# A new order for the first 220 tasks of a fused FFT convolution and gated MLP, with later transposes of the inverse tables and another order of staging buffers

## The chip, the cores and the metric

The kernel runs on one core of one Trainium2 chip. The core has a matrix engine (PE), a vector engine (DVE), an activation engine (ACT), a general engine (POOL) and a queue engine (SP) that here does nothing but issue transfers; ACT issues some as well. Each engine works through its own list of instructions in order, and they wait for each other by semaphores. The metric is the device time of one execution in microseconds; the kernel before took 194.77 us (median of three runs).

## The reference

All tensors are bfloat16, with 2048 positions of 512 channels. Two branches work on the same normalised input and are multiplied.

```
x  = A_q;  xn = layernorm(x)
k_shift = sum over t in 0..3 of k moved by t places * shift_k     # 4-tap causal filter per channel
kv = k_shift * v
y  = irfft( rfft(kv, 4096) * rfft(ssm_k, 4096) )[:2048] + kv * ssm_D
s  = xn * y
h  = gelu(xn @ w_gate) * (xn @ w_up)                              # 512 -> 1792
g  = silu(h @ w_down)                                             # 1792 -> 512
out = x + s * g
```

## The kernel before

The long convolution is a discrete Fourier transform in two stages, both done by matrix products. Stage 1 multiplies 128-point tables (F1) with the data, PE's results are evacuated into staging buffers and stored to scratch arrays in DRAM (ZH for the filter ssm_k, ZK for kv). Stage 2 reads them back in another layout (tiles BH and BK), multiplies by a second table (TF) in 32-by-32 blocks (line 1028), multiplies the two spectra (HS, HW), applies the inverse tables (MI, its halves MI0 and MI1, made from TFA and TFB) and goes back through a third scratch array (ZI) to the last stage with the table G1.

The filter is split in two halves. The first, called H in the code, is transposed on PE (line 878, from the tiles Hn) into HTr, and its units 4 to 7 are worked in half pairs of 256 columns. Its evacuated results lie in four quarters of the tile X, which later takes the input, and ACT issues the eight stores. The second half, called J, comes from a permuted copy (HP, by ACT) and a transposing DMA (HTD); SP issues its stores. Its four staging buffers are quarters of X and of G, the tile in which the output is made later. kv is built on DVE: four products of k with the filter taps (lines 1005 and 1009) and three sums (line 1011) for each of four blocks. The taps (SKB) are four copies by POOL out of one loaded tile (SKR).

The MLP works in four quarters of 512 tokens. Each quarter has 14 units; a unit is a gate and an up product (xnT with Wg and Wu), a GELU on ACT (GE, line 1137, or 1128 for a 256-column piece) and a product on DVE (HT, line 1140, or 1130). The first quarter starts with two halves of 256 columns, while weights and input are still landing. The normalised input XN is made on DVE (line 835), transposed on PE (line 854) and evacuated by ACT as xnT (line 609).

The order of all this is written out by hand. Every piece of work is a task with a number, given when it is added. The string SEQ lists 787 places with the numbers, and the planner goes through it exactly in that order and puts each task on the list of its engine. The planner also reckons times from constants (LANDS, W_XT and the costs of the tasks). These times do not change the order. They only decide which slot of a pool of buffers a task gets, by the earliest free one. On the chip an engine waits for semaphores alone.

Loads, stores and transposing transfers issued by SP all stand in one list, so an entry that waits holds up everything behind it. The transposing transfers for G1 and the two tables share one semaphore, so each waits until the one before it has landed. Lines that the prediction names: line 609 is the copy by ACT out of PSUM, line 618 the matmul, line 590 the plain transfer, line 1039 the transposing transfer of the tables.

Of the kernel before, what the change touches and what calls it, by code (L numbers as in the profile page):

```python
# [24 lines left out]
N_WARM = 11  # L25
ORDER = "x02 h0 h1 x22 w0 w1 h2 h3 D0 w2 s0 k0 v0 x1 w3 k1 v1 d0 d1 k2 v2 k3 v3 x2 x3"
SEQ = (
# [22 lines left out]
)  # L50
NF_BANKS = 4
ISSUE = 470.0
LOAD_NS = {("x0_", 262144): 1400.0, ("x0_", 131072): 450.0, 262144: 900.0, 524288: 1350.0, ("x", 524288): 2100.0, ("h", 524288): 1300.0, ("wg", 524288): 1550.0, ("wu", 524288): 1450.0, 917504: 2620.0, ("sk", 524288): 1500.0, 344064: 1250.0, 46080: 350.0, 3072: 100.0, 1024: 200.0}
W_XT, W_SW, W_BK, W_BH, W_ZI, W_BI, W_ZK, W_MI, W_G1 = 1665000, 600000, 555000, 703000, 333000, 640000, 490000, 740000, 222000
NC_PAIRS = 4
SMALL = 1.15 * 262144
T_FWD = 219.0
# [234 lines left out]
class Sched:  # L292
# [8 lines left out]
    FIRST = {"loads": 1050.0, "SP": 30500.0}  # L301
    DRAIN = 121.0
    EARLY, TAKEN, SHARED, WAIT = (0.0, 1.0), 1400.0, 46000.0, 3300.0
    LANDS = (4350.0, 5590.0, 7100.0, 8420.0, 9350.0, 10200.0, 11500.0)

    def __init__(self):
        self.tasks = []
# [37 lines left out]
    def run(self):  # L345
        free = dict(self.FIRST)
        pipe = 0.0
        n_loads = 0
        order = []
        pmode = 0  # L350
        for name in SEQ.split():
            t = self.tasks[int(name.rstrip("b"))]
            eng, dur = t.opts[name[-1] == "b"]
            base = 0.0
            for d in t.deps:
                base = max(base, d.end if eng == d.eng == "PE" else d.end + d.lat + (self.SEM if not d.nbytes or eng != "PE" else 400.0 if d.eng == "loads" else self.HEDGE))
            for b in t.w:
                if b.pool is not None and b.slot is None:
                    f, b.slot = b.pool.find()
                    b.pool.take(b.slot)  # L360
                    base = max(base, f + self.SEM)
            t.start, t.eng = max(base, free.get(eng, 800.0)), eng
            free[eng] = t.end = t.start + dur + (self.DRAIN if eng == "PE" and t.mode != pmode else 0.0)
            pmode = t.mode if eng == "PE" else pmode
            if eng == "loads":
                free[eng] = t.start + dur * (self.EARLY[1] if t.start < self.EARLY[0] else 1.0)
                if n_loads < len(self.LANDS):
                    free[eng] = self.LANDS[n_loads] - self.LOAD_LAT
                n_loads += 1
                t.end = free[eng] + self.LOAD_LAT  # L370
            elif t.nbytes:
                en = t.end
                if en < self.SHARED:
                    free["loads"] += self.TAKEN
                pipe = max(pipe, en + self.DMA_LAT / 2) + t.nbytes / (self.SHARE_BW if en < self.SHARED else self.DMA_BW)
                t.end = pipe + self.DMA_LAT / 2 + (self.WAIT if en < self.SHARED else 0.0)
            for b in set(t.r + t.w):
                b.left -= 1
                b.last_end = max(b.last_end, t.end + t.lat)
                if b.left == 0 and b.pool is not None:  # L380
                    b.pool.release(b.slot, b.last_end)
            order.append(t)
        assert sorted(t.n for t in order) == list(range(len(self.tasks)))
        return order
# [6 lines left out]
def act(n, sb=False):  # L391
    return 170.0 + n * 0.833 + (30.0 if sb else 0.0)


def dve(n, rate):
    return 150.0 + n / 0.96 / rate


def build_kernel(nc, A_q, A_k, A_v, A_shift_k, A_ssm_k, A_ssm_D, B_w_gate, B_w_up, B_w_down, out):
    with ExitStack() as es0:  # L400
# [81 lines left out]
        def quarter(T, j):  # L482
            return T[:, j:j + 2, :].rearrange("p x (y d) -> p (x y) d", d=256).rearrange("p (r c) d -> p r c d", c=2)

        ast = {"H": [quarter(X, j) for j in (8, 10, 12, 14)], "J": [quarter(T, j) for T, j in ((X, 12), (X, 14), (G, 4), (G, 6))],
               "K": [AST[:, j, :, :, :] for j in range(2)] + [ASX[:]]}

        ZH = nc.dram_tensor("ZH", [NG, 128, DM], BF16, kind="Internal")
# [402 lines left out]
        d_htd = [dsem(f"d_htd{hf}") for hf in range(2)]  # L891
        for hf in range(2):
            for k in range(2):
                h_perm.append(op([("ACT", act(1024, True)), ("DVE", dve(1024, 1))], lambda e, h, hf=hf, k=k: copy(e, h, HP[:, 8 * hf:8 * hf + 8, k, :], Hn[:, 2 + k, :].rearrange("p (a t) -> p t a", t=NT)[:, 8 * hf:8 * hf + 8, :]),
                                 r=[bHn[2 + k]], w=[bHP[hf]], rr=[R_Hn[2 + k]], ww=[R_HP[hf]]))
        for hf in range(2):
            def dtr(e, hf=hf):
# [31 lines left out]
        def stage1_h(x, u):  # L929
# [9 lines left out]
            else:  # L939
# [6 lines left out]
                def m(e):  # L946
# [3 lines left out]
                s1_tasks[x].append(S.add([("PE", pe(2))], m, r=[bF1] + bd, w=[p], lat=200.0))  # L950
                form = "p (c d r) -> p r c d" if x == "H" else "p (c r d) -> p r c d"
                op(EV(1024), lambda e, h: copy(e, h, ast[x][a.slot], ps(psl(p)).rearrange(form, c=2, r=2)),
                   r=[p], w=[a], rr=lambda: R_ps[psl(p)], ww=lambda: [R_AST[x][a.slot]], after=[] if x == "H" else zh_tasks["H"])
            zh_tasks[x].append(S.add([("ACT", 350.0) if x == "H" else ("SP", ISSUE)], st, r=[a], w=[bZ["H"][u + (8 if x == "J" else 0)]], nbytes=1.05 * SMALL))

        def stage1_k(u):
# [330 lines left out]
```

## Time and profile before

| what | value |
|---|---|
| three runs | 194.37, 194.77, 195.28 us (median 194.77) |
| span of the profiled execution | 193.3 us; the median of the runs is 1.47 us longer |
| instructions | 3502 |
| PE busy | 188.6 us, 98% of the span |
| DVE busy | 160.0 us, 83% |
| ACT busy | 125.4 us, 65% |
| POOL busy | 13.9 us, 7% |

The profiled execution is one more execution beside the three runs; its page gives its span. A row of a timeline gives the start in us, the time from the start of its first to the end of its last instruction, the engine, the line, the operation, what is written and what is read, and how many instructions there are; brackets give the idle time before it and what ended that. "ACTq" and "SPq" are the issues of transfers on those engines' lists, and the row of a transfer in the list of issues ends with the time from issue to landing. A row of the windows view gives a stretch, then the busy time of PE, weight load, DVE, ACT and POOL in it, the granted clock of PE, the share of the transfer engines and GB/s.

### The profile page before, as it was taken

How to read it: one execution, taken by the hardware profiler on the slowest of the kernel's cores; microseconds unless marked ns; L12 is line 12 of the kernel's file. 1: busy time of each engine (PE TensorE's matmuls, PEld its weight loads, DVE VectorE, ACT ScalarE, POOL GpSimd, SP SyncE). 2: the span in 40 equal slices, each digit the busy share in tenths (PEclk: the TensorE clock that was granted, in tenths of full speed). 3: DMA queues.
4: the chain of work that ended last, by engine and by line, in shares of the span. 5: the costliest groups of instructions: out<-in, count | busy, mean ns of one | idle time of the engine just before them, and what ended most of it. 6: DMA issues, size and time to landing. Idle time of an engine off the chain costs nothing.

```text
span 193.3 us, 3502 instructions
## 1 busy us (share of the span) xinstructions
PE 188.6 (98%) x1377; PEld 85.6 (44%) x1377; DVE 160.0 (83%) x245; ACT 125.4 (65%) x170; POOL 13.9 (7%) x32
## 2 busy tenths in 40 slices
PE   7899999999999999999999999999999999999993
PEld 2685544444444444443434433433444334444452
DVE  6699789998999995877888789878897863588993
ACT  6787999969885987868548766856577431232121
POOL 5412420000000000020300000000000000000000
PEclk9999999999999999999999999999999999999999
DMA  5999999999999679999999991984805345939333
GB/s 175 311 307 349 377 400 347 157 249 372 375 374 354 196 264 259 390 323 305 218 285 230 338 320 59 288 276 147 264 10 195 106 140 153 389 112 353 132 139 136
DMA packets 45958, 49.19 MB, mean 254 GB/s; under 512 B 12787, under 2 KB 39671, under 8 KB 45942
## 3 DMA queue, kind: packets, MB, share of 16 engines
q1 hardware_dynamic: 37366, 42.67, 70.1%
q10 hardware_dynamic: 8576, 6.29, 10.3%
q8 instruction: 11, 0.18, 0.4%
q14 instruction: 5, 0.04, 0.1%
HBM read 27.39 MB, written 14.68 MB: 218 GB/s over the span
## 4 chain that ended last, share of the span: by engine, by line
PE 93%; DMA 4%; SPq 1%; DVE 1%; ACT 0%; issue 0%
PE psall L618 86%; PE psall L1028 5%; DMA Hn<-in_A_ssm_k_dram 4%; PE psall L854 1%; SPq L590 1%; PE psall L878 1%; DVE G L1175 0%; DVE G L1174 0%; ACT G L1172 0%
## 5 line engine op out<-in xcount | busy, mean ns | idle before, releaser
L618 PE MATMUL psall<-xnT,Wu 128*128 128x512 bf16 (+1 forms) x232 | 55.8, 372 | 0.0
L618 PE MATMUL psall<-xnT,Wg 128*128 128x512 bf16 (+1 forms) x232 | 55.3, 372 | 0.0
L618 PE MATMUL psall<-Wd,HT 128*128 128x512 bf16 (+2 forms) x238 | 52.0, 367 | 0.0
L1140 DVE TENSOR_TENSOR HT<-psall,GE 128x512 bf16<-128x512 f32 x54 | 36.7, 685 | 15.8 <-PE psall L618 15.4
L1137 ACT ACTIVATE GE<-psall 128x512 bf16<-128x512 f32 x54 | 31.7, 601 | 13.1 <-PE psall L618 12.9
L618 PEld LDWEIGHTS psall<-Wd,HT 128*128 128x128 bf16 x238 | 22.4, 98 | 25.9 <-issue 1.1
L618 PEld LDWEIGHTS psall<-xnT,Wg 128*128 128x128 bf16 x232 | 21.9, 98 | 25.4 <-issue 1.3
L618 PEld LDWEIGHTS psall<-xnT,Wu 128*128 128x128 bf16 x232 | 21.6, 98 | 25.9 <-issue 3.5
L609 ACT ACTIVATE X<-psall 128x1024 bf16<-128x1024 f32 (+1 forms) x18 | 15.1, 843 | 3.3 <-DMA ZH<-X 1.9
L609 ACT ACTIVATE HS<-psall 128x1024 bf16<-128x1024 f32 x14 | 13.7, 1022 | 4.4 <-PE psall L1028 4.4
L1164 ACT ACTIVATE G<-psall 128x512 bf16<-128x512 f32 x12 | 7.0, 598 | 12.9 <-PE psall L618 12.4
L1011 DVE TENSOR_TENSOR KAC<-KAC,KTM 128x2048 bf16<-128x2048 bf16 x12 | 14.6, 1217 | 0.1
L1009 DVE TENSOR_TENSOR KTM<-KK,SKB 128x2048 bf16<-128x2048 bf16 x12 | 14.6, 1217 | 0.0
L609 ACT ACTIVATE BO<-psall 128x1024 bf16<-128x1024 f32 x9 | 9.1, 1022 | 8.2 <-PE psall L1028 7.7
L609 ACT ACTIVATE KB<-psall 128x1024 bf16<-128x1024 f32 x11 | 11.0, 1021 | 3.6 <-PE psall L1028 3.6
L609 ACT ACTIVATE AST<-psall 128x1024 bf16<-128x1024 f32 x12 | 12.4, 1033 | 0.7 <-PE psall L618 0.5
L612 DVE CAST BO<-psall 128x1024 bf16<-128x1024 f32 x7 | 8.5, 1224 | 3.7 <-PE psall L1028 3.7
L821 DVE BATCH_NORM_STATS2 stats<-X 128x6 f32<-128x512 bf16 x16 | 10.3, 675 | 1.1 <-DMA X<-in_A_q_dram 1.1
L1172 ACT ACTIVATE G<-psall 128x512 bf16<-128x512 f32 (+2 forms) x5 | 2.6, 512 | 13.1 <-PE psall L618 13.1
L1091 DVE TENSOR_TENSOR HW<-KB,HW 128x1024 bf16<-128x1024 bf16 x16 | 10.9, 682 | 0.0
L1091 DVE TENSOR_TENSOR HS<-KB,HS 128x1024 bf16<-128x1024 bf16 x16 | 10.8, 682 | 0.0
L1166 DVE SCALAR_TENSOR_TENSOR G<-G,psall 128x512 bf16<-128x512 bf16 x12 | 7.8, 680 | 2.0 <-ACT G L1164 2.0
(83 smaller groups left out, 175.6 us busy)
## 6 DMA issues: line engine op xcount, KB each, us to landing
BH<-ZH SPq DMA_DIRECT2D x8, 512.0 KB, 6.1
HW<-HS SPq DMA_DIRECT2D x16, 256.0 KB, 3.2
BK<-ZK SPq DMA_DIRECT2D x8, 512.0 KB, 5.1
ZI<-BO ACTq DMA_DIRECT2D x16, 256.0 KB, 2.8
BI<-ZI SPq DMA_DIRECT2D x8, 512.0 KB, 4.2
ZK<-AST SPq DMA_DIRECT2D x6, 512.0 KB, 4.1
Hn<-in_A_ssm_k_dram SPq DMA_DIRECT2D x4, 512.0 KB, 8.4
KK<-in_A_k_dram SPq DMA_DIRECT2D x4, 512.0 KB, 8.6
```

The source lines that it names most:

```text
L609: return h.activation(o, i, ACTF.Copy, scale=scale)
L612: return h.tensor_copy(o, i)
L618: return h.matmul(o, lhsT=l, rhs=r, start=st, stop=sp)
L821: t_stats[t] = op([("DVE", 670.0)], lambda e, h, t=t: h.bn_stats(stats[:, t, :], X[:, t, :]), r=[bX[q][t % 4]], w=[bst[t]], rr=[R_X[t]], w ...
L1009: op([("DVE", dur)], lambda e, h, j=j, m=m: h.tensor_tensor(KTM[:, m.slot, :, :], kk(j), sk(j), ALU.mult), r=need + [bSKB[j], a], w=[m], r ...
L1011: op([("DVE", dur)], lambda e, h, m=m: h.tensor_tensor(KAC[:, a.slot, :, :], KAC[:, a.slot, :, :], KTM[:, m.slot, :, :], ALU.add), r=[m], ...
L1028: trk.op("PE", lambda h: h.matmul(ps(s, i)[b, :], lhsT=wt(col)[a, :], rhs=data(col)[a, :], start=n < 16, stop=n >= len(todo) - 16, tile_po ...
L1091: return hd.tensor_tensor(o, flat(KB, kb[h]), o, ALU.mult)
L1137: op([("ACT", act(512))], lambda e, h: h.activation(GE[:, g.slot, :], bank(pg), ACTF.Gelu_apprx_tanh), r=[pg], w=[g], rr=lambda: R_bank(pg ...
L1140: op([("DVE", dve(512, 1))], lambda e, h: h.tensor_tensor(HT[:, q % 2, m, :], bank(pu), GE[:, g.slot, :], ALU.mult), r=[pu, g], w=[bHT[q][m]],
L1164: op([("ACT", act(n))], lambda e, h, g=g, pc=pc: h.activation(g, pc(), ACTF.Tanh, scale=0.5), r=[p], w=[bt], rr=lambda p=p: R_bank(p), ww= ...
L1166: op([("DVE", dve(512, 1))], lambda e, h, g=g, pc=pc: h.scalar_tensor_tensor(out=g, in0=g, scalar=1.0, in1=pc(), op0=ALU.add, op1=ALU.mult ...
```

## The change

The first 220 places of SEQ are written anew. Behind them the list is the same, except that the transposes of the two tables come later: MI0 (task 183) goes from place 252 to 331 and MI1 (task 184) from 295 to 342, both from ahead of G1 (task 182, place 316 before and 314 after) to behind it. The order of the second half's staging buffers is turned round, so that the two quarters of G are taken first. The evacuations of that half no longer have to come after the first half's stores in the plan. Three things change in the planner's reckoning: LANDS goes by bytes, the weight of a transposing load goes down and the permuting copies cost 2000 ns on ACT. Of the list itself the diff shows the ends of the first line only.

```diff
-    "17 18 0 3 1 2 4 8 5 7 11 20 6 9 50 12 65 66 67 73 19 68 75 74 49 10 76 13 52 21 82 22 86 117 83 ..."
+    "3 17 0 1 8 11 4 12 5 6 2 9 18 20 10 13 7 50 19 21 22 36 23 49 31 27 24 25 67 68 51 65 75 66 32 ..."
...
-W_XT, W_SW, W_BK, ... = 1665000, 600000, 555000, ...
+W_XT, W_SW, W_BK, ... = 1400000, 600000, 555000, ...
...
-    LANDS = (4350.0, 5590.0, 7100.0, 8420.0, 9350.0, 10200.0, 11500.0)
+    LANDS = ((0.0, 2300.0), (262144.0, 3700.0), ..., (3145728.0, 14500.0))
...
-                if n_loads < len(self.LANDS):
-                    free[eng] = self.LANDS[n_loads] - self.LOAD_LAT
-                n_loads += 1
+                n_loads += t.nbytes
+                for (b0, t0), (b1, t1) in zip(self.LANDS, self.LANDS[1:]):
+                    if b0 < n_loads <= b1:
+                        free[eng] = t0 + (t1 - t0) * (n_loads - b0) / (b1 - b0) - self.LOAD_LAT
...
-        ast = {"H": [...], "J": [quarter(T, j) for T, j in ((X, 12), (X, 14), (G, 4), (G, 6))],
+        ast = {"H": [...], "J": [quarter(T, j) for T, j in ((G, 4), (G, 6), (X, 12), (X, 14))],
...
-                h_perm.append(op([("ACT", act(1024, True)), ("DVE", dve(1024, 1))], ...
+                h_perm.append(op([("ACT", 2000.0), ("DVE", dve(1024, 1))], ...
...
-                   r=[p], w=[a], rr=..., ww=..., after=[] if x == "H" else zh_tasks["H"])
+                   r=[p], w=[a], rr=..., ww=...)
```

The first place is the start of PE. The rows of `HTr` with 256 columns are half pairs of stage 1, two matmuls each; the rows of Hn are the filter's transposes, the second of which works on the second Hn tile. Before:

```order
L878 MATMUL psall<-ident_63,Hn 128x128 x8
L854 MATMUL psall<-ident,XN 128x128 x4
L618 MATMUL psall<-HTr,F_58 128x256 x2
L854 MATMUL psall<-ident,XN 128x128 x4
L618 MATMUL psall<-HTr,F_58 128x256 x4
L878 MATMUL psall<-ident_63,Hn 128x128 x8
L618 MATMUL psall<-xnT,Wg 128x256 x4
L618 MATMUL psall<-HTr,F_58 128x256 x2
L854 MATMUL psall<-ident,XN 128x128 x4
```

After, at the same place and on to the third piece of the transposes of the next quarter, which are the XN rows further down (line numbers are two higher):

```order
L880 MATMUL psall<-ident_63,Hn 128x128 x8
L856 MATMUL psall<-ident,XN 128x128 x4
L620 MATMUL psall<-HTr,F_58 128x256 x4
L856 MATMUL psall<-ident,XN 128x128 x4
L620 MATMUL psall<-HTr,F_58 128x256 x4
L880 MATMUL psall<-ident_63,Hn 128x128 x8
L620 MATMUL psall<-xnT,Wg 128x256 x4
L856 MATMUL psall<-ident,XN 128x128 x4
L620 MATMUL psall<-HTr,F_58 128x256 x4
L620 MATMUL psall<-xnT,Wu 128x256 x4
L856 MATMUL psall<-ident,XN 128x128 x4
L620 MATMUL psall<-xnT,Wg 128x256 x4
```

One half pair of the first filter tile moved ahead of the second tile's transposes, and the product with the second piece of XN came forward behind them.

The second place is DVE where the first product of kv (KAC) starts. The XN rows belong to the next quarter, the HT rows to the MLP. Before:

```order
L835 TENSOR_SCALAR XN<-X,mv 128x512 x2
L1140 TENSOR_TENSOR HT<-psall,GE 128x512
L835 TENSOR_SCALAR XN<-X,mv 128x512
L1140 TENSOR_TENSOR HT<-psall,GE 128x512
L835 TENSOR_SCALAR XN<-X,mv 128x512
L1140 TENSOR_TENSOR HT<-psall,GE 128x512
L1005 TENSOR_TENSOR KAC<-KK,SKB 128x2048
L1140 TENSOR_TENSOR HT<-psall,GE 128x512
L1009 TENSOR_TENSOR KTM<-KK,SKB 128x2048
```

After:

```order
L837 TENSOR_SCALAR XN<-X,mv 128x512 x3
L1142 TENSOR_TENSOR HT<-psall,GE 128x512 x2
L1007 TENSOR_TENSOR KAC<-KK,SKB 128x2048
L837 TENSOR_SCALAR XN<-X,mv 128x512
L1011 TENSOR_TENSOR KTM<-KK,SKB 128x2048
L1132 TENSOR_TENSOR HT<-psall,GE 128x256
L1013 TENSOR_TENSOR KAC<-KAC,KTM 128x2048
```

The last XN of the quarter, XN5 in the list, moved from ahead of KAC to behind it.

The third place is the list of SP from the end of the loads to the first read of the filter (BH). Before:

```order
L590 DMA ZH<-G 128x4x256
L1039 DMA_TRANSPOSE G_59<-F_58 128x2x128
L590 DMA ZH<-G 128x4x256
L590 DMA ZH<-X 128x4x256
L590 DMA ZK<-ASX 128x2048
L590 DMA ZH<-X 128x4x256
L590 DMA ZK<-AST 128x2048 x2
L590 DMA X<-in_A_q_dram 128x2048
L590 DMA BH<-ZH 128x4x512
```

After:

```order
L592 DMA ZH<-X 128x4x256
L1041 DMA_TRANSPOSE G_59<-F_58 128x2x128
L592 DMA ZH<-X 128x4x256
L592 DMA ZH<-G 128x4x256
L1041 DMA_TRANSPOSE MI<-TFA 128x8x128
L592 DMA ZK<-ASX 128x2048
L592 DMA ZH<-G 128x4x256
L1041 DMA_TRANSPOSE MI<-TFB 128x8x128
L592 DMA ZK<-AST 128x2048 x2
L592 DMA X<-in_A_q_dram 128x2048
L592 DMA BH<-ZH 128x4x512
```

Both transposes of the tables moved from further up in this list to behind G1, and the second now stands four rows ahead of the first BH.

On ACT's list the first of its eight stores ZH stood behind four GELUs of 256 columns and one of 512, and now stands behind two of 256 columns. On POOL the four copies of the taps run in the order 3, 0, 1, 2 where they ran 3, 2, 1, 0.

More of the change, by code (lines that the diff above doesn't have):

```diff
@@ L53 @@
 LOAD_NS = {("x0_", 262144): 1400.0, ("x0_", 131072): 450.0, 262144: 900.0, 524288: 1350.0, ("x", 524288): 2100.0, ("h", 524288): 1300.0, ("wg", 524288): 1550.0, ("wu", 524288): 1450.0, 917504: 2620.0, ("sk", 524288): 1500.0, 344064: 1250.0, 46080: 350.0, 3072: 100.0, 1024: 200.0}
-W_XT, W_SW, W_BK, W_BH, W_ZI, W_BI, W_ZK, W_MI, W_G1 = 1665000, 600000, 555000, 703000, 333000, 640000, 490000, 740000, 222000
+W_XT, W_SW, W_BK, W_BH, W_ZI, W_BI, W_ZK, W_MI, W_G1 = 1400000, 600000, 555000, 703000, 333000, 640000, 490000, 740000, 222000
 NC_PAIRS = 4
@@ L303 @@
     EARLY, TAKEN, SHARED, WAIT = (0.0, 1.0), 1400.0, 46000.0, 3300.0
-    LANDS = (4350.0, 5590.0, 7100.0, 8420.0, 9350.0, 10200.0, 11500.0)
+    LANDS = ((0.0, 2300.0), (262144.0, 3700.0), (786432.0, 5050.0), (1048576.0, 7550.0), (1572864.0, 8950.0), (1835008.0, 9800.0), (2097152.0, 10650.0), (2621440.0, 12100.0), (3145728.0, 14500.0))
     def __init__(self):
@@ L347, in run @@
         pipe = 0.0
-        n_loads = 0
+        n_loads = 0.0
         order = []
@@ L483, in quarter @@
             return T[:, j:j + 2, :].rearrange("p x (y d) -> p (x y) d", d=256).rearrange("p (r c) d -> p r c d", c=2)
-        ast = {"H": [quarter(X, j) for j in (8, 10, 12, 14)], "J": [quarter(T, j) for T, j in ((X, 12), (X, 14), (G, 4), (G, 6))],
+        ast = {"H": [quarter(X, j) for j in (8, 10, 12, 14)], "J": [quarter(T, j) for T, j in ((G, 4), (G, 6), (X, 12), (X, 14))],
                "K": [AST[:, j, :, :, :] for j in range(2)] + [ASX[:]]}
@@ L893, in build_kernel @@
             for k in range(2):
-                h_perm.append(op([("ACT", act(1024, True)), ("DVE", dve(1024, 1))], lambda e, h, hf=hf, k=k: copy(e, h, HP[:, 8 * hf:8 * hf + 8, k, :], Hn[:, 2 + k, :].rearrange("p (a t) -> p t a", t=NT)[:, 8 * hf:8 * hf + 8, :]),
+                h_perm.append(op([("ACT", 2000.0), ("DVE", dve(1024, 1))], lambda e, h, hf=hf, k=k: copy(e, h, HP[:, 8 * hf:8 * hf + 8, k, :], Hn[:, 2 + k, :].rearrange("p (a t) -> p t a", t=NT)[:, 8 * hf:8 * hf + 8, :]),
                                  r=[bHn[2 + k]], w=[bHP[hf]], rr=[R_Hn[2 + k]], ww=[R_HP[hf]]))
@@ L952, in stage1_h @@
                 op(EV(1024), lambda e, h: copy(e, h, ast[x][a.slot], ps(psl(p)).rearrange(form, c=2, r=2)),
-                   r=[p], w=[a], rr=lambda: R_ps[psl(p)], ww=lambda: [R_AST[x][a.slot]], after=[] if x == "H" else zh_tasks["H"])
+                   r=[p], w=[a], rr=lambda: R_ps[psl(p)], ww=lambda: [R_AST[x][a.slot]])
             zh_tasks[x].append(S.add([("ACT", 350.0) if x == "H" else ("SP", ISSUE)], st, r=[a], w=[bZ["H"][u + (8 if x == "J" else 0)]], nbytes=1.05 * SMALL))
```

45 rows, old and new, of the table SEQ are left out of this document.

## The prediction

> **What bounds the kernel now.** I read the engine totals first, then the chain that ended last.
>
> ```profile
> PE 188.6 (98%) x1377; PEld 85.6 (44%) x1377; DVE 160.0 (83%) x245; ACT 125.4 (65%) x170; POOL 13.9 (7%) x32
> 2.12 7.16 DMA Hn<-in_A_ssm_k_dram
> 12.28 11.48 PE psall L618 x68
> 81.42 0.36 PE psall L1028 x16
> 157.37 32.18 PE psall L618 x152
> ```
>
> PE is busy for 98% of the span and holds the chain from where Hn has landed (9.28 us): its first long piece starts at 12.28, its last ends at 189.55 (157.37 + 32.18), and all between is PE's. Both kernels issue the same matmuls, so a new order can only win what PE idles before 12.3 us, and it loses whatever new idle time it makes behind that point. Hence the start of PE, row by row:
>
> ```profile
> 7.18 0.39 PE L854 MATMUL psall<-ident,XN 128*128 128x128 bf16 x4
> 7.82 0.39 PE L618 MATMUL psall<-HTr,F 128*128 128x256 bf16 x2 [0.25 <-ACT HTr L609]
> 8.04 0.39 PE L854 MATMUL psall<-ident,XN 128*128 128x128 bf16 x4
> 8.27 0.60 PE L618 MATMUL psall<-HTr,F 128*128 128x256 bf16 x4
> 9.32 1.16 PE L878 MATMUL psall<-ident,Hn 128*128 128x128 f32 x8 [0.46 <-DMA Hn<-in_A_ssm_k_dram]
> 10.32 0.60 PE L618 MATMUL psall<-xnT,Wg 128*128 128x256 bf16 x4
> 10.82 0.39 PE L618 MATMUL psall<-HTr,F 128*128 128x256 bf16 x2
> 11.23 0.38 PE L854 MATMUL psall<-ident,XN 128*128 128x128 bf16 x4
> 13.86 1.04 PE L618 MATMUL psall<-xnT,Wu 128*128 128x256 bf16 x8
> 14.73 0.38 PE L618 MATMUL psall<-HTr,F 128*128 128x256 bf16 x2
> 16.04 2.75 PE L618 MATMUL psall<-xnT,Wg 128*128 128x512 bf16 x12
> 18.63 1.89 PE L618 MATMUL psall<-xnT,Wu 128*128 128x512 bf16 x8
> ```
>
> From start to start a matmul takes 0.109 us at 256 columns (13.86 to 14.73, eight of them) and 0.216 us at 512 (16.04 to 18.63, twelve); four bf16 transposes take 0.22 us (8.04 to 8.27). The profiled execution has a span of 193.3 us, 1.47 us under the median of 194.77. I make the sum against the span and add the 1.47 back.
>
> **The start: -0.47 us.** The loads of the first 29 places of SP stay in their order, so the second filter tile (Hn) should still land at 9.28 us (2.12 + 7.16), and its eight transposes should still start at 9.32. Ahead of them PE now does four half pairs of stage 1 instead of three: two more 256-column matmuls, 0.22 us of work that moves into the 0.46 us wait. They fit, for 7.82 + 0.44 + 0.22 + 0.44 is 8.92 us. Behind the transposes before idles 0.06 us (10.32 + 0.44 is 10.76, next start 10.82) and 0.19 us (10.82 + 0.22 is 11.04, next start 11.23). After has other work there whose inputs are older, so I take both away: 0.25 us. Together 0.47. Its ends: all of it goes if ACT, which now evacuates nearly back to back from 7.66 to about 13.6 us, delivers late (0), and no more can be had than the three (-0.5). I take -0.47, since the new row's inputs are ready earlier than PE.
>
> **Stores that overtake loads: +0.7 us.** The new list gives the filter stores (ZH) to ACT's queue earlier. In after the first stands behind ten evacuations and two narrow GELUs, which from the 7.82 at which ACT has done its first one, at up to 0.6 us each (603 ns for one) and with some overlap, puts it at about 13.65 us; the second follows the second wide GELU, at about 17.0 us; the third comes near 21.8 us.
>
> ```profile
> L609 ACT ACTIVATE xnT<-psall 128x512 bf16<-128x512 bf16 x8 | 4.7, 603 | 0.6 <-PE psall L854 0.5
> 17.11 0.38 ACTq L590 DMA_DIRECT2D ZH<-X  x1
> 21.57 0.37 ACTq L590 DMA_DIRECT2D ZH<-X  x1
> 16.00:18.00 2.00, 2.00 (x12) 0.93 (x11) 2.00 (x10) 1.25 (x4) 0.82 (x2) 1.00 1.07 316
> q1 hardware_dynamic: 726, 0.86, 78.9%
> q10 hardware_dynamic: 504, 0.25, 27.9%
> ```
>
> Before issued its first two at 17.11 and 21.57. The stretch from 16 to 18 us shows a DMA share of 1.07, so the transfer engines are full and a store can only go at the cost of loads. The two queue rows are of 20.5 to 23.5 us, when one store was moving: q10, ACT's, took 27.9% of 3 us, 0.84 us of all 16 engines. By about 21.6 us after has sent one whole store more than before. So loads that land between 17.5 and 25 us come up to 0.84 us later. Two of them have nothing to spare:
>
> ```profile
> Wu<-in_B_w_up_dram SPq DMA_DIRECT2D x1, 512.0 KB, 11.4
> KK<-in_A_k_dram SPq DMA_DIRECT2D x1, 512.0 KB, 10.9
> 6.18 1.02 SPq L590 DMA_DIRECT2D Wu<-in_B_w_up_dram  x1
> 12.38 0.41 SPq L590 DMA_DIRECT2D KK<-in_A_k_dram  x1
> 23.32 1.42 DVE L1005 TENSOR_TENSOR KAC<-KK,SKB 128x2048 bf16<-128x2048 bf16 x1
> 24.66 0.68 DVE L1140 TENSOR_TENSOR HT<-psall,GE 128x512 bf16<-128x512 f32 x1
> 21.23 0.40 DVE L835 TENSOR_SCALAR XN<-X,mv 128x512 bf16<-128x512 bf16 x1
> ```
>
> The landings are those of the single issue in each row's moment: the second up-weight piece at 6.18 + 11.4, 17.58 us, and the first k tile at 12.38 + 10.9, 23.28 us. In after PE's rows between Hn's transposes and the first 512-column up product are 40 of 256 columns, 12 of 512 and two groups of transposes: 4.36 + 2.59 + 0.44 is 7.39, so PE gets there at 10.32 + 7.39, 17.71 us, with 0.13 us of slack before any delay. The second is new in kind. The third normalised tile (XN5) of the next quarter stood ahead of the first k product (KAC, line 1005) on DVE and now stands behind it; KAC waits for the k tile. Up to the transposes of XN5 PE has 40 matmuls of 256 columns, 46 of 512 and three groups of transposes from 10.32 on: 4.36 + 9.94 + 0.66 more, which is 25.28 us. With k at 23.28: KAC from 23.32, the next DVE start 1.34 us later, 0.40 for XN5 and 0.1 to pass it on make 25.16, 0.12 us ahead of PE. With k 0.84 us later it is 26.0, and PE waits 0.7 us. A stall at the up weights would be the same slip taken earlier, and then XN5 is in time: it is paid once. The ends are 0 (packets of the added store hit other loads) and 0.84 + 0.3 (KAC slowed again and a second store counted in part). I take the 0.84 less the 0.12 that was spare, 0.7, nearer to the upper end because the engines show no room in the stretch above.
>
> Behind it the shift carries over: the third up piece and the permutes of the filter (HP) then have the same 0.7 us more. I cost them at nothing.
>
> **Order of the four coefficient copies on POOL: 0.** The second product now waits for the copy that goes last.
>
> ```profile
> L986 POOL COPY SKB<-SKR x4: 637/646/1658, 21.9 to 23.6; 128x512 bf16<-128x512 bf16 x4
> 27.45 0.69 DVE L1140 TENSOR_TENSOR HT<-psall,GE 128x512 bf16<-128x512 f32 x1 [0.94 <-PE psall L618]
> ```
>
> The last copy, started at 23.6 beside the product at 23.32, took 1658 ns where the others took about 646. It ends at 25.3, up to 0.8 us later if its source lands later too. The GELU products behind the waiting product on DVE free PE's banks, so a delay there reaches PE in the end; but at 27.45 DVE stood idle for 0.94 us waiting for PE, which takes up 0.8. The ends are 0 and 0.8, and I take 0 by that idle time. [...]
>
> **The inverse tables' transposes and the buffers: 0.** The tables (MI0, MI1) and G1 share one semaphore, so each waits until the one before has landed.
>
> ```profile
> 44.33 5.69 SPq L1039 DMA_TRANSPOSE MI<-TFA  x1
> 54.57 2.61 SPq L1039 DMA_TRANSPOSE MI<-TFB  x1
> 64.01 0.36 SPq L590 DMA_DIRECT2D ZH<-X  x1
> 72.62 0.74 SPq L590 DMA_DIRECT2D BH<-ZH  x1
> MI<-TFA SPq DMA_TRANSPOSE x1, 10.2
> MI<-TFB SPq DMA_TRANSPOSE x1, 6.2
> G<-F SPq DMA_TRANSPOSE x1, 2.9
> BH<-ZH SPq DMA_DIRECT2D x1, 512.0 KB, 7.2
> ```
>
> MI0 moves from 44.33 us, where it held SP for 5.69, to behind the seventh store of the second filter half, which before issued at 64.01: so to about 64.4 us. MI1 then waits for MI0 and stands straight ahead of two K stores, a load and the first filter read (BH). That read lands at 79.8 us (72.62 + 7.2) and PE needs it at 81.42: 1.6 us of slack. If MI0 lands L after 64.4 and MI1 holds SP for 2.6 us as it did, and the three issues between take 0.36 each, BH goes at 68.1 + L, which is L - 4.5 later than before. Up to L = 6.1 nothing is lost. G1 (two 128-column blocks where the tables have eight), the nearest in time, landed in 2.9 us; MI1 in 6.2; MI0 in 10.2, behind k, v and Wd loads in the same queue, which at 64 us are gone. I take L between 2.9 and 6.2, cost 0; the ends are 0 and +4.1 us (10.2 less 6.1). The exchange of staging (G before X) lets two stores of the second half go out beside MI0's old place, and no PE wait there depends on them: 0, with an issue of 0.36 us as the price either way.
>
> [...]
>
> Sum: 193.3 - 0.47 + 0.7 + 0 + 0 = 193.5, plus 1.47 gives 195.0 us.
>
> **Rivals.**
> - The start's gain is kept: the extra store falls on loads that have room, and PE's idle time is gone. For it speaks that each load shares the engines with several others (726 packets of q1 in the row above are those of more than one). 194.77 - 0.47 is 194.3. Chance 0.22.
> - Slower through MI0: L over 6.1, BH late. From 7 to 10.2 us it costs 0.9 to 4.1 us on top of the forecast: 195.9 to 199.1. For it speaks MI0's 10.2, against it that the loads it queued behind are gone. It decides from L = 6.1 on. Chance 0.13.
> - Slower through further small waits in 13 to 40 us, where DVE and ACT are nearly full (2.00 of 2.00 us on DVE in the row above) and a permute of the filter now stands ahead of evacuations: the 0.7 once or twice again, 195.7 to 196.4. Chance 0.10.
> - Nothing moves: the list changes the order but ACT is late by what PE saves, 194.8. Chance 0.08.
>
> **How the numbers follow.** The forecast, 195.0 (194.6 to 195.6 by itself), has 0.47. About 0.5% (0.97 us: 193.80 and 195.74) is what a measurement of this kernel can tell from no change. Faster than 193.80 would need more than the idle time of the start: 0.06, from a mis-sized chain. Slower than 195.74: nearly all of the two slower rivals, 0.23 less 0.03, and 0.03 of the forecast's edge, 0.23. The rest, 0.71, is within. The range leaves out the long end of the MI0 rival and the little below 194.0: 194.0 to 196.4.
>
> **What would show it.** Right: eight fp32 transposes at 9.3 us with four half pairs ahead, no PE gap from 10.3 to 17 us; the second up piece landing at 18 us or later, or a PE gap of 0.5 to 0.7 us at 17.7 or at 25.3; the k tile at 24 us; then PE dense to the end, BH landing before PE's first tiled product. Wrong: Hn landing at another time than 9.3 us; MI1 issued past 71 us and a gap ahead of the first L1028 product; PE gaps between 26 and 60 us.

## The result and the profile after

The changed kernel takes 196.20 us (median of six runs, 195.51 to 197.68), the kernel before 194.57 us in the runs beside it. The ratio is 1.0105, with a 95% interval of 1.0069 to 1.0142: slower by about 1%, where the prediction had 195.0 us and no change that can be measured. The time lies near the upper end of the range that it gave (194.0 to 196.4 us), but a mechanism that it did not have put it there.

The profiled execution has a span of 194.6 us and took 196.43. These are the totals and the shares of the chain that ended last, from the page of the kernel after:

```profile
PE 188.0 (97%) x1377; PEld 84.9 (44%) x1377; DVE 161.0 (83%) x246; ACT 124.5 (64%) x169; POOL 14.1 (7%) x32
PE 79%; DMA 13%; DVE 4%; POOL 1%; ACT 1%; issue 0%; SPq 0%; DVEq 0%; ACTq 0%
```

PE does the same work, but now transfers hold 13% of the chain. From the same chain, the middle, and from the timeline of PE the only two rows behind 12 us that show idle time:

```profile
11.06 12.15 DMA KK<-in_A_k_dram
23.30 1.45 DVE KAC L1007
24.75 0.66 DVE XN L837
25.45 0.40 PE psall L856 x4
33.20 16.79 PE psall L620 x78
49.99 9.86 DMA ZH<-G
59.93 1.03 ACT G L611
61.01 21.76 PE psall L620 x100
25.45 0.40 PE L856 MATMUL psall<-ident,XN 128*128 128x128 bf16 x4 [0.74 <-DVE XN L837]
61.01 0.60 PE L620 MATMUL psall<-V,F 128*128 128x512 bf16 x2 [1.47 <-ACT G L611]
```

The first wait, 0.74 us, is the one the prediction named: XN5 behind KAC behind the k tile. The second, 1.47 us, it did not name. The second filter half has four staging buffers, so its fifth evacuation by ACT waits until the first store out of these buffers has landed. That store was issued at 49.99 us and landed 9.86 us later, at 59.84. PE's next product waited for this evacuation (59.93 + 1.02) and started at 61.01 us. On ACT it reads:

```profile
35.20 2.15 ACT L611 ACTIVATE HP<-Hn 128x1024 bf16<-128x1024 bf16 x1
59.93 1.02 ACT L611 ACTIVATE G<-psall 128x1024 bf16<-128x1024 f32 x1 [3.19 <-DMA ZH<-G]
```

In the profile of before the same wait stands on ACT with 0.96 us, and PE had none:

```profile
57.87 1.02 ACT L609 ACTIVATE X<-psall 128x1024 bf16<-128x1024 f32 x1 [0.96 <-DMA ZH<-X]
```

There the store landed at 57.8 us. So the store comes 2 us later in the new order. The windows view (columns as described for the page above, DMA share and GB/s last) shows where those transfers lost time. First the kernel after, then the kernel before in a second profile of it:

```profile
34.00:36.00 2.00, 2.00 (x11) 0.88 (x10) 2.00 (x3) 2.00 (x3) 0.00 (x0) 1.00 1.01 201
36.00:38.00 2.00, 2.00 (x11) 0.88 (x9) 2.00 (x4) 2.00 (x3) 0.00 (x0) 1.00 0.03 8
32.00:40.00 8.00, 8.00 (x42) 3.75 (x41) 8.00 (x10) 7.72 (x12) 0.00 (x0) 1.00 0.65 138
```

```profile
36.00:38.00 2.00, 2.00 (x11) 0.88 (x10) 1.74 (x3) 2.00 (x5) 0.00 (x0) 1.00 0.88 196
32.00:40.00 8.00, 7.95 (x38) 3.72 (x38) 7.74 (x9) 7.86 (x11) 0.00 (x0) 1.00 1.07 209
```

From 36 to 38 us the transfer engines of the kernel after stand still (share 0.03), and from 32 to 40 us they move 138 GB/s where before moves 209 (200 in its first profile, at a share of 0.97). SP's list waits there for the second transposing load of the filter (HTD), which waits for the last permute (HP) on ACT. That permute starts at 35.20 us; in the second profile of before it starts at 33.50, in the first at 33.79. The permute ahead of it starts at nearly the same time in either order. First the second profile of before, then the row of after that goes with the 35.20 above:

```profile
29.64 2.09 ACT L609 ACTIVATE HP<-Hn 128x1024 bf16<-128x1024 bf16 x1 [0.24 <-DMA Hn<-in_A_ssm_k_dram]
33.50 2.10 ACT L609 ACTIVATE HP<-Hn 128x1024 bf16<-128x1024 bf16 x1
29.92 2.09 ACT L611 ACTIVATE HP<-Hn 128x1024 bf16<-128x1024 bf16 x1 [0.36 <-DMA Hn<-in_A_ssm_k_dram]
```

So it is the new list of ACT that makes the last permute late: six instructions stand between the two permutes, where three stood. From 40 to 60 us the engines are full in both (share 1.05 and 1.08), so what was lost is not made up there.

### The profile page after: what moved, and what is told of

It is laid out like the page before. It is cut to its first block, busy times and chain, and to the rows that moved or that the text cites. A ratio compares the mean times of both kernels' runs of the same rounds, so it can differ in the third digit from the quotient of the medians.

```text
span 194.6 us, 3503 instructions
## 1 busy us (share of the span) xinstructions
PE 188.0 (97%) x1377; PEld 84.9 (44%) x1377; DVE 161.0 (83%) x246; ACT 124.5 (64%) x169; POOL 14.1 (7%) x32
## 4 chain that ended last, share of the span: by engine, by line
PE 79%; DMA 13%; DVE 4%; POOL 1%; ACT 1%; issue 0%; SPq 0%; DVEq 0%; ACTq 0%
PE psall L620 74%; DMA KK<-in_A_k_dram 6%; PE psall L1030 5%; DMA ZH<-G 5%; DMA X<-in_A_q_dram 2%; DVE XN L837 1%; DVE KAC L1007 1%; DVE stats L823 1%; DVE HTr L614 1%; POOL mv L834 1%; ACT G L611 1%; PE psall L856 0%; DVE G L1177 0%; DVE G L1176 0%; SPq L592 0%
## 5 line engine op out<-in xcount | busy, mean ns | idle before, releaser
L611 ACT ACTIVATE X<-psall 128x512 bf16<-128x512 f32 (+1 forms) x14 | 11.0, 808 | 0.8 <-PE psall L620 0.8
L620 PE MATMUL psall<-V,F 128*128 128x512 bf16 x32 | 9.2, 379 | 1.5 <-ACT G L611 1.5
```

The costliest lines, as they stand in the source:

```text
L611: return h.activation(o, i, ACTF.Copy, scale=scale)
L620: return h.matmul(o, lhsT=l, rhs=r, start=st, stop=sp)
```

## The experiments

The repeated kernel and 14 variants were run, each beside the kernel before, with these times (medians; ratio to before; the landing of the first store of the second half and the span are those of the profiled execution, which is not always one near the median):

| run | time us | ratio, 95% interval | landing | span | span - landing |
|---|---|---|---|---|---|
| before (first profile) | 194.77 | | 57.8 | 193.3 | 135.5 |
| b_again | 194.51 | 0.9999 (0.9987 to 1.0011) | 57.8 | 192.6 | 134.8 |
| before_mi_late | 194.63 | 1.0015 (0.9999 to 1.0031) | 56.3 | 192.7 | 136.4 |
| before_stage_new | 194.37 | 0.9995 (0.9974 to 1.0015) | 58.1 | 193.2 | 135.1 |
| before_zh2_late | 194.84 | 1.0030 (1.0009 to 1.0051) | 57.7 | 192.5 | 134.8 |
| before_hp_late | 197.31 | 1.0137 (1.0105 to 1.0169) | 61.7 | 196.5 | 134.8 |
| before_idle | 197.08 | 1.0124 (1.0095 to 1.0153) | 62.3 | 197.1 | 134.8 |
| after | 196.20 | 1.0105 (1.0069 to 1.0142) | 59.8 | 194.6 | 134.8 |
| xn5_first | 196.74 | 1.0109 (1.0090 to 1.0127) | 60.0 | 194.9 | 134.9 |
| after_mi_old | 197.81 | 1.0173 (1.0133 to 1.0212) | 60.9 | 195.7 | 134.8 |
| after_stage_old | 196.85 | 1.0142 (1.0108 to 1.0176) | 60.0 | 194.8 | 134.8 |
| zh2_early | 196.43 | 1.0090 (1.0062 to 1.0118) | 60.2 | 195.0 | 134.8 |
| zh21_early | 195.84 | 1.0060 (1.0039 to 1.0081) | 58.3 | 193.2 | 134.9 |
| zh21_xn5 | 195.58 | 1.0055 (1.0032 to 1.0078) | 58.8 | 194.0 | 135.2 |
| hp1_early | 196.93 | 1.0110 (1.0091 to 1.0129) | 58.7 | 196.2 | 137.5 |
| both | 197.12 | 1.0127 (1.0108 to 1.0146) | 57.8 | 195.0 | 137.2 |
| zh21_hp1_xn5 | 195.91 | 1.0069 (1.0042 to 1.0096) | 57.3 | 194.7 | 137.4 |

The last column carries the study. In the seven runs where PE's last wait for work is that for this store, the span is the landing plus 134.8 us, within 0.1, from a landing of 59.8 to one of 62.3 us. Where PE is late for another reason, the difference is larger. Three runs have 134.8 or 134.9 without a row of PE that shows the wait. In zh21_early PE does wait, for less than 0.2 us, as told below. In b_again and before_zh2_late PE comes just as the evacuation ends (at 58.92 us in b_again, with PE's next product at 59.00).

**The kernel before again.** No edit.

> The kernel before once more, to see which part of its profile is chance. If the late second Hn tile (landed at 9.28 us in before, at 7.97 us in after, with the same loads in the same order) belongs to the order, it lands at 9.3 us again and the span is about 193.3 us. If it is a matter of one execution, it lands near 8 us, PE starts about 1 us earlier, and the span is 192.3 to 193.3 us. The time is 194.6 us either way, within 0.4 us.

The time is the same. The second Hn tile landed at 8.25 us and not at 9.28. It did so in all runs of the study: 7.9 to 8.5 us in either order. The late tile was a matter of that one execution.

**XN5 ahead of KAC again** (463 is XN5, 150 the first KAC):

```diff
-  401 147 403 150 415 99 469 409 463 100 151
+  401 147 403 463 150 415 99 469 409 100 151
```

> The changed kernel with XN5 ahead of KAC on DVE again, nothing else. Theory A (the end is set by the landing of the first store of the second filter half, near 59.8 us, for which ACT's fifth evacuation and then PE wait): the wait of 0.74 us at 25.4 us is gone, the wait at 61.0 us grows from 1.47 to 2.2 us, and the time stays at 196.2 us within 0.3. Theory B (each wait adds to the time by itself): 0.74 us faster, 195.5 us.

```profile
61.40 0.38 PE L620 MATMUL psall<-V,F 128*128 128x512 bf16 x1 [2.11 <-ACT G L611]
```

The wait at 25 us is gone and the one at 61 us is 2.11 us. The time did not fall (196.74 against 196.20, intervals overlapping). Theory A holds, theory B falls: the first wait is paid out of the second.

**The last permute earlier, alone and with XN5** (60 is the permute, 470 an evacuation):

```diff
-  466 470 97 155 425 427 420 60 156
+  466 470 60 97 155 425 427 420 156
```

> The changed kernel with the last permute of the filter (HP) two evacuations earlier on ACT, about where the kernel before had it. Theory A: the second transposing load of the filter goes about 1.4 us earlier, all behind it on SP lands 1 to 2 us earlier, the first store of the second half at 57.8 to 58.8 us instead of 59.8, the wait at 61 us falls from 1.47 to under 0.5 us, and the time to 194.7 to 195.2 us. Theory C (the late landing comes from the other staging order or from the transposes of the tables): landing and time as in the changed kernel, 196.2 us.

> The changed kernel with both of these moves. Theory A: no wait at 25 us, a wait of 0.5 to 1.2 us left near 60 us because PE comes earlier and the landing does not; time as with the earlier permute alone, 194.5 to 195.0 us. Theory B: the two gains add up, 2.2 us, to 194.0 us.

The landing moved as expected, to 58.7 and 57.8 us, but the time did not, and both forecasts missed. With the permute alone a new wait stands in its place, on PE and on ACT:

```profile
57.66 0.60 PE L620 MATMUL psall<-V,F 128*128 128x512 bf16 x2 [1.99 <-ACT X L611]
56.58 1.02 ACT L611 ACTIVATE X<-psall 128x1024 bf16<-128x1024 f32 x1 [2.82 <-DMA ZH<-X]
```

This evacuation goes into a quarter of X that still held a result of the first half. Its store, one of those that ACT issues from 40.7 us on, landed at 56.5 us, behind the loads that SP had queued in the meantime (in the changed kernel these stores landed at 43 to 55 us). So the permute's place and the stores' places belong together. With both moves PE waited at four places between 44 and 65 us for 0.17 to 0.71 us, 1.84 us in all, where the changed kernel waits 2.21 at two.

**Tables and staging, in both kernels.** In the changed kernel the two tables go back to their old places (183 behind 140, 184 behind 137); in another the buffers go back to X first; the kernel before gets each part by itself:

```diff
-  ... 139 183 237 238 ... 124 184 249
+  ... 140 183 45 ... 137 184 241
...
-  "J": [quarter(T, j) for T, j in ((G, 4), (G, 6), (X, 12), (X, 14))]
+  "J": [quarter(T, j) for T, j in ((X, 12), (X, 14), (G, 4), (G, 6))]
```

> The changed kernel with the transposes of both tables at their old places, MI0 ahead of the last k tile and of the first stores. Theory A: MI0 takes about 0.9 us of the queue there (in before 54.56 against 53.69 us for the transfer ahead of it), so the first store of the second half lands near 60.7 us and the time goes up by 0.9, to 197.1 us. Theory C, that the later transposes cost time: 1 us faster, 195.2 us.

> The changed kernel with the staging buffers in their old order, X before G. Theory A: the fifth evacuation of the second half waits for the first store in whichever buffer it lies, so landing, wait and time stay, 196.2 us within 0.3. Theory C, that the order of the buffers makes the wait: the wait at 61 us is gone and the time is 194.8 us.

> The kernel before with the transposes of both tables at their new places behind G1, nothing else. Theory A: the first store of the second half lands about 0.9 us earlier and nothing waits for the 0.9, the first read of the filter goes about 1 us later within its 1.6 us of slack: 194.6 us within 0.3. Theory C: 1 us or more slower, 195.6 us.

> The kernel before with the staging buffers in the new order, G before X, nothing else. Theory A: no change, 194.6 us within 0.3. Theory C: a wait of PE near 60 us appears and the time is about 1 us longer, 195.6 us.

By themselves neither part changes the kernel before: 1.0015 and 0.9995. With the tables at their old places the changed kernel's ratio is higher (1.0173 against 1.0105, with intervals that still overlap a little), the landing is at 60.9 us, near the 60.7 of theory A, and the wait is 2.19 us. In before_mi_late the store landed 1.5 us earlier and nothing came of it, since PE was not waiting. The old staging order leaves the landing at 60.0 us and the time within the spread of the changed kernel's; PE waits 1.05 us at 53 us, for a buffer of X, and 0.43 us at 61. Theory C falls.

**Stores earlier** (97 evacuates filter unit 2, 98 stores it; 95 stores unit 1, 423 is a GELU). First 98 alone, then 95 too, then with the permute and XN5:

```diff
-  470 97 155 ... 408 98 429
+  470 97 98 155 ... 408 429
...
-  422 423 472 ... 41 95 157
+  422 423 95 472 ... 41 157
```

> The changed kernel with one of ACT's stores (the 256 KB of filter unit 2) issued right behind its evacuation, near 35 us, and not with another one near 39.3 us. Theory D (the transfer engines run dry from 36 to 38 us, share 0.03, because the permute and a store stand later on ACT; all transfers behind come later by what was idle): the share from 36 to 38 us rises to 0.4 to 0.5, the first store of the second half lands 0.5 to 0.9 us earlier, near 59.2 us, the wait of PE at 61 us falls from 1.5 to 0.6 to 1.0 us, and the time to 195.6 us. Rival (the late landing comes from the competition of ACT's stores with SP's loads, not from idle time): moving a store earlier changes nothing, 196.3 us.

> The same with the store of filter unit 1 moved as well, from 40.6 to about 33 us (its result is in the buffer since 29 us). Theory D: share from 32 to 38 us near full, the first store of the second half lands 1.2 to 1.7 us earlier than in the changed kernel, near 58.4 us, the wait at 61 us is 0 to 0.5 us, the time 194.7 to 195.2 us. Rival: 196.3 us.

> The changed kernel with all four moves: both stores and the last permute earlier, XN5 ahead of KAC. Theory D: no idle time of the transfer engines between 32 and 40 us, the filter's stores out of X landed by 52 us so that the wait of the earlier-permute run at 57 us is gone too, no wait of PE over 0.5 us from 12 us on; time 194.0 to 194.6 us, that of the kernel before or a little less. Rival: as with the permute and XN5 alone, 197.1 us.

One store alone missed. The timeline of ACT in that run shows why:

```profile
34.26 1.02 ACT L611 ACTIVATE X<-psall 128x1024 bf16<-128x1024 f32 x1
35.31 0.37 ACTq L592 DMA_DIRECT2D ZH<-X  x1
35.72 0.60 ACT L1139 ACTIVATE GE<-psall 128x512 bf16<-128x512 f32 x1 [0.44 <-PE psall L620]
36.21 2.07 ACT L611 ACTIVATE HP<-Hn 128x1024 bf16<-128x1024 bf16 x1
```

The store could be issued only when the evacuation ahead of it had ended (34.26 + 1.02), and the next GELU began 0.04 us after the issue (35.31 + 0.37). The profile puts these 0.44 us of idle time down to PE; the same gap at the same place in the next run, where PE was earlier, speaks for the issue, which is an inference. With a landing of the last Hn tile that was 0.4 us later in this execution, the permute went from 35.20 to 36.21 us. The share from 32 to 40 us was 0.64, as little as before the move. With two stores the stretch fills up, and the wait at 61 us is gone:

```profile
32.00:40.00 8.00, 8.00 (x42) 3.75 (x40) 7.99 (x9) 7.56 (x11) 0.00 (x0) 1.00 0.88 193
58.38 1.02 ACT L611 ACTIVATE G<-psall 128x1024 bf16<-128x1024 f32 x1 [1.87 <-PE psall L620]
55.82 1.03 PE L620 MATMUL psall<-HTD,F 128*128 128x512 bf16 x4
58.41 1.03 PE L620 MATMUL psall<-xnT,Wg 128*128 128x512 bf16 x4
59.46 0.60 PE L620 MATMUL psall<-V,F 128*128 128x512 bf16 x2
```

The landing is 58.3 us, as forecast. The row of ACT names PE, but PE's product for this evacuation (HTD) had ended by 56.85 us, and the evacuation starts 0.08 us behind the landing as in the changed kernel (59.85 and 59.93). So ACT still waits for the store. PE's next product starts 0.06 us behind the evacuation's end (59.40), about 0.2 us later than four matmuls from 58.41 on take (4 times the 0.216 of the prediction). The wait has shrunk from 1.47 to about 0.2 us, which is why this run too has 134.9 in the last column.

This run also tells what sets the landing. The last permute stands later here than in the changed kernel (35.77 us), and the first load behind the second HTD is issued later (40.11 against 39.19 us), yet the store lands 1.5 us earlier (in zh21_xn5, below, 1.0 us earlier with the permute at 35.66 us). So a later permute does not by itself make the landing late. What counts, by these two runs, is how much the engines have moved by then (193 against 138 GB/s from 32 to 40 us).

The ratio falls to 1.0060, with an interval that overlaps that of the changed kernel at its end. The median of 195.84 us is 0.6 above the forecast's upper end; its runs spread from 194.95 to 196.68. With all four moves the landing is early (57.3 us), and PE now waits for GELUs that stand behind the permutes:

```profile
33.12 1.04 PE L620 MATMUL psall<-xnT,Wg 128*128 128x512 bf16 x4 [0.47 <-ACT GE L1139]
38.52 1.04 PE L620 MATMUL psall<-xnT,Wg 128*128 128x512 bf16 x4 [0.43 <-ACT GE L1139]
```

Only the second of these GELUs stands behind the moved permute (34.39 us). The first stands behind the other permute, for whose tile ACT waited 1.48 us, until 30.48.

**The other way round: the idle time put into the kernel before.** The permute (60) two GELUs later, the store (98) beside the last ones, and both. The places 62 and 44 move along with the permute; on SP the second HTD and the load behind it keep their order.

```diff
-  93 60 62 431 44 425 426 427 428
+  93 431 425 426 427 60 62 44 428
...
-  419 98 420 ... 499 95
+  419 420 ... 499 98 95
```

> The kernel before, with only the last permute (HP) two GELUs later on ACT and the store of filter unit 2 beside the last three, which makes the changed kernel's idle time in the old order. Theory D: share from 36 to 38 us under 0.2, the first store of the second half lands 1.5 to 2.5 us later than 57.8 us, PE waits 0.8 to 1.8 us near 60 us, time 195.4 to 196.4 us. Rival (the new order of the first 12 us or of PE is what costs): 194.6 us.

> The kernel before with only the last permute (HP) two GELUs later on ACT. Theory D (what counts is how much the transfer engines move from 32 to 40 us): the second transposing load goes 1.5 to 2.8 us later, the share from 32 to 40 us is 0.75 to 0.9 (0.97 in before, 0.62 with both moves), the first store of the second half lands at 59.5 to 61 us, the time is 195.2 to 196.5 us. If the store alone is the cause: 194.6 us.

> The kernel before with only the store of filter unit 2 moved from 36.1 to about 40 us, beside the last ones. Theory D: 256 KB less in the stretch from 32 to 40 us, share 0.8 to 0.9, the first store of the second half lands 0.5 to 0.9 us later, near 58.5 us, and the time is 194.6 to 195.3 us. If the permute alone is the cause: 194.6 us.

In the kernel before with the permute late alone, from the windows, SP's timeline, PE's and ACT's:

```profile
38.00:40.00 2.00, 1.88 (x10) 0.68 (x9) 1.19 (x2) 2.00 (x4) 0.00 (x0) 1.00 0.16 35
32.00:40.00 8.00, 7.83 (x38) 3.49 (x37) 6.85 (x8) 6.59 (x10) 0.00 (x0) 1.00 0.77 151
38.56 2.32 SPq L899 DMA_TRANSPOSE HTD<-HP  x1
62.83 0.60 PE L618 MATMUL psall<-V,F 128*128 128x512 bf16 x2 [2.13 <-ACT X L609]
61.75 1.02 ACT L609 ACTIVATE X<-psall 128x1024 bf16<-128x1024 f32 x1 [3.56 <-DMA ZH<-X]
```

One instruction of ACT moved behind two GELUs makes the old kernel 1.4% slower (197.31 us, 0.8 more than the top of the forecast; with both moves 197.08, 0.7 more than its top), with the changed kernel's signs: engines idle before 40 us, the store landing at 61.7 us, PE waiting 2.1 us for it. In this execution PE also waited 0.87 us at 25.6 us for a load of up weights, ahead of the edit; the permute ahead of the moved one still started at 29.99 us, so the late permute does not come from that. The store moved alone does little: landing 57.7 us, ratio 1.0030. So in the old order the permute, through the transposing load that waits for it, is what matters, and not the store.

**Stores earlier and XN5 first:**

> The changed kernel with the two stores earlier and XN5 ahead of KAC, the permute left where it is. Theory A: the wait at 25 us (0.65 us with the two stores alone) is gone; the first store still lands near 58.3 us, so PE, which comes 0.65 us earlier, waits 0.3 to 0.8 us for it again, and the time is 195.2 to 195.9 us, no better than with the stores alone (195.84). If the waits simply add up: 195.2 us or less.

The edits are those shown above. The wait at 25 us is gone, one of 1.24 us stands at 60.2 us, and the time is not told apart from that with the stores alone (1.0055 against 1.0060). No version tried is faster than the kernel before.

## Why the prediction was wrong, point by point

- **The base and the start (-0.47 us).** Here the row was read rightly and the execution was not typical. The second Hn tile, at 9.28 us in that profile, landed at 7.9 to 8.5 us in all later ones, so the 0.46 us wait ahead of its transposes was not there to fill (one of the old list's other profiles has 0.29 us, the rest none). PE's time from 5.5 to 12 us beyond its work, summed from the starts of its matmuls, is 2.2 us in that profile, 1.1 to 1.5 in the old list's others and 1.0 to 1.7 in the new list's. The term is not told apart from zero. The 1.47 us between span and time goes with this: every later pair gives 1.8 (196.43 less 194.6 here), so that profile was of an execution of about 195.1 us.
- **Stores that overtake loads (+0.7).** The stores were issued at 12.72, 16.33 and 20.65 us, each about 1 us ahead of the forecast. But the k tile landed at 23.22 us against 23.15 in the repeat of before, not 0.84 later. The wait for XN5 came all the same (0.74 us), because PE was there at 24.7 us and not at 25.28. That its size came out as forecast is luck. The up piece that the prediction took at 17.58 us landed at 15.63 (16.06 in the repeat of before), so nothing was tight there. The wait was worth nothing: xn5_first and zh21_xn5 take it away and the time stays.
- **Behind it: "the permutes of the filter (HP) then have the same 0.7 us more. I cost them at nothing."** This is the step that failed, together with "no PE wait there depends on them: 0" on the second half's stores. No shift of 0.7 us carried over: the first of the last two permutes started as before (29.92 us), and the second came 1.4 to 1.7 us later than in the two profiles of before (35.20 against 33.79 and 33.50), by the new list of ACT. It held up the transposing load. The transfer engines ran dry (share 0.03 from 36 to 38 us), and the first store of the second half landed 2 us later, for which PE waits by way of ACT: 1.47 us in place of 0. The page of before showed ACT waiting for these stores, 1.9 us in two waits, and the prediction did not follow these waits on to PE. PE had only 0.7 us to spare behind them in that profile (135.5 less 134.8) and none in the repeat.
- **The exchange of staging: 0.** Right: 0.9995 in the old kernel.
- **The coefficient copies: 0.** Right. The copies took 654 to 1653 ns, and the second product began at 25.32 us straight behind XN5.
- **The tables: 0.** Right. MI0 landed 3.3 us after its issue, within the 2.9 to 6.2 taken, and MI1 held SP for 1.34 us. In the old kernel the move gives 1.0015. In the changed kernel it seems to hide part of the loss (1.0173 with the old places).
- **The rivals.** None of them was it. "Further small waits in 13 to 40 us" had about the right time (195.7 to 196.4) and the right engine, ACT with its permute, but the wrong mechanism: behind 26 us and up to 40 PE has no wait there, it waits ahead of 61.01 us. Two of the signs that were to show the forecast wrong did come: Hn landed at another time than 9.3 us, and PE had a gap from 59.5 us on, at the end of the stretch from 26 to 60 us.

What is not settled: no edit brought the changed kernel back to the old time. The late permute by itself makes the old order slow, but taking it away in the new order (hp1_early, both) only trades this wait for others, so it is not shown that the permute is the whole of the 1% there. It is also open why the median of zh21_early stays 0.6% above before with a span of 193.2 us in its profile (a run of 194.95 us); the runs spread by 1.7 us, and only one was profiled.

## What to carry to other kernels

Follow every small wait for a store on an off-path engine to its end: here a staging buffer that was used again tied an evacuation, and by it PE (1.47 us), to a landing at 59.8 us that idle transfer engines some 20 us earlier (share 0.03 from 36 to 38 us) had made late. Where a kernel's transfer engines are full for a long stretch, as here from 40 to 60 us (share 1.05), cost the moments in which the queue runs dry and not only the bytes that move: here the first store behind such a moment landed 2 us later (59.8 against 57.8 us). And before a term is built on one row of one execution, ask whether that row is the order's or that execution's.

## What the runs showed of the hardware

A transposing load of the filter moved fewer bytes in a microsecond than loads and stores did, with the transfer engines full in both stretches (share 1.27 and 1.05). In the profile of before, 1 us in which a transposing load ran alone, and a stretch with loads and stores:

```profile
34.90:35.90 1.00, 1.00 (x6) 0.44 (x5) 1.00 (x2) 1.00 (x2) 0.00 (x0) 1.00 1.27 287
48.00:50.00 2.00, 2.00 (x11) 0.92 (x10) 2.00 (x3) 1.83 (x3) 0.00 (x0) 1.00 1.05 401
```

They moved 287 and 401 GB/s. The share adds up the times of the packets, and in these rows it passes 1: per share it is 226 against 382 GB/s. The packets differ too (0.29 MB in 1121 packets, about 256 bytes each, against 0.80 MB in 508), so the rows do not tell the transposing from the small packets.

Where ACT issued a store right behind its own evacuation, it sat idle for 0.44 us in zh2_early (from 35.28 to 35.72 us) and for 0.44 us in zh21_early (from 34.83 to 35.27 us): the time from the end of the evacuation to the end of the issue and 0.04 us more. The rows put that time down to PE, so that the store costs it is an inference.
